# Receptance input in buffers of its own during attention, two probability tiles, and another order of the mixer's first weights

## Chip, cores and metric

The kernel runs on one core of a Trainium2 chip. The metric is the device time of one execution in microseconds (us); several runs give a median. One further execution was profiled.

## What is computed

Three parts follow each other. Attention over 4 batches, 8 heads, 576 positions, head size 64, in which scores more than tau below the row's largest are dropped. A channel mix (RWKV's feed-forward) with 512 and 1024 channels. A spectral mixer: a two-dimensional Fourier transform, its real part added, a layer norm and a two-layer feed-forward with 2048 hidden channels.

```python
scores = scale * np.matmul(q, k.transpose(0, 1, 3, 2))
thresh = np.max(scores, axis=-1, keepdims=True) - tau
attn = softmax(np.where(scores >= thresh, scores, -1e9)) @ v
...
xk = mu_k * x + (1.0 - mu_k) * x_prev      # x_prev: x of the position before
xr = mu_r * x + (1.0 - mu_r) * x_prev
k = np.maximum(xk @ w_k, 0.0)
x = sigmoid(xr @ w_r) * (k * k @ w_v)
...
u = x + real(fft(fft(x, axis=1), axis=2))
out = u + np.maximum(layernorm(u) @ w_ch1, 0.0) @ w_ch2
```

## The kernel before

Attention works on 16 pairs of heads, 4 pairs for each batch, with 9 steps for each pair. A step has scores on TensorE (PE, `s`, L218 and L232), the row's largest on VectorE (DVE, L258), the exponential on ScalarE (ACT, L269), the selection and its sum on DVE (L273), the normalization on GpSimd (POOL, L281), transposes on PE (`t`, L320 and L328, and `tm`, L340 and L343, for the step that holds the remainders), and copies of the transposed probabilities from PSUM into a probability tile `pt` on ACT (L323, L347). A tile `pt` holds one half (288 positions) of a pair; the pool keeps three of them. When a half is complete, the product with the values runs on PE (`av`, L379), and its result becomes a piece of `xT`.

The feed-forward works on halves of a batch: `ffn_stream` is a generator with, for every half, 8 key tiles (`kps`, L399 to L401, 96 matmuls), 4 receptance tiles (`rps`, the same lines, 48 matmuls), 4 value tiles (`vps`, L511 to L513, 96 matmuls), and the transposes of the result of the half before (`xn`, L529), which stand between `kps` and `rps`. Every product is three matmuls, of high and low parts. The inputs are made by `build_xs`: for each of 4 chunks a multiplication on POOL (L423), a multiply-add on DVE (L424, `xtmp`), the high part on ACT (L425, `xh`) and the low part on POOL (L427, `xl`; a few on DVE). There is one buffer each for `xh` and `xl`, and key and receptance inputs take turns in it. The call only queues the chunks in `builds`; they are written into the program two at a time, once in each attention step.

`do_X` pulls the stream in every attention step as far as a credit allows. A scheduler then orders all instructions of each engine by data, buffers and priorities, so the order on an engine is not that of the source. Feed-forward of batches 0 to 2 lies between the steps of attention, that of batch 3 follows attention, beside the Fourier transforms of the first batches and the conversion of the mixer's weights.

The mixer's weights come in four quarters (`quarter`, tiles `cA` and `cB` in turn), each as 8 pieces of `w_ch1` and 8 of `w_ch2`, which are loaded by POOL's queue and split into high and low parts by DVE (L67 to L69), ACT (L72) and POOL (L73). `w_ch1` lies so that a piece holds, for one of four k, the hidden channels of two of four f; product f of `ch1` (`c1ps`, L949 to L951) needs pieces of all four k.

Of the kernel before, what the change touches and what calls it, by code (L numbers as in the profile page):

```python
# [9 lines left out]
F32 = mybir.dt.float32  # L10
F32R = mybir.dt.float32r
# [8 lines left out]
D, FF, FC = 512, 1024, 2048  # L20
HS = S // 2
NPAIR = H // 2
P = dict(PRI=100, SR=1.0, CR=2, ORD=0, PF=0, CB=0, XT=0, XL=0, K2=0, FE=0, FE3=0, MU=0, WP=256, C1=2, RB=4, BB=2, FT=4, A0=[7, 8], A1=[11, 12], B0=[7, 8], B1=[11, 12], PT4=1, OR0='', XH=0, SP0=0, CA=1.48, CN=2.22, QS=1, pF=100, pM=100, pN=100, pT=100, pO=100, pE=100, pS=100, pA=0, pX=0, NA=0, LT=2, WS=3, WR=1, CC=3.0, BN=2, OR='FATXOESBI', TM=8, SO=0, SO0=0, AO=0, AO0=0, QS0=0, XD=0, TH=0, SM=0, SM0=0, N0=34, qF=100, qM=100, qN=100, qT=100, qO=100, qE=100, qS=100, qA=100, qX=30, RQ=[0,0,0,0,0,0,0,0], XN=0, QN=36, AVR=0, LX=2, WD=0, WP2=512, E3=1, NA0=0, W0=0, XD2=0, PO=0, WP1=512, IN=[0,1,2,2,4,5,6,7])
# [5 lines left out]
def tile_kernel(ctx: ExitStack, tc: tile.TileContext, a):  # L29
# [48 lines left out]
    def whole(pair, base=0):  # L78
        return lambda c, n: [x[:, c - base:c - base + n] for x in pair]
# [6 lines left out]
    def big(slot, name):  # L86
        return wA.tile([128, 4096], F32R, tag=slot, name=name)
# [3 lines left out]
    wr = [wC.tile([128, 2048], F32R, name=f"wr{i}") for i in range(2)]  # L91
# [3 lines left out]
    at = astack.enter_context(tc.tile_pool(name="at", bufs=1, side="right"))  # L95
# [32 lines left out]
    def settle():  # L128
        go, second[:] = list(second), []
        for f in go:  # L130
            f()
        while pending:
            pending.pop(0)()
# [4 lines left out]
    heads, vts, ptu, ptr, et, em, sps, stat, xT = ({} for _ in range(9))  # L138
# [128 lines left out]
    def emit_exp(n):  # L267
        st = stat[n]
        act.activation(two(eview(n)), sps[n][:, :, 0:HS], AF.Exp, bias=st[:, 0:1])  # L269
# [27 lines left out]

    def unit(pi, half):
        if (pi, half) not in ptu:
            ptu[pi, half] = at.tile([128, 2, 4, HS], F32, tag="pt", bufs=3, name="pt")  # L300
        return ptu[pi, half]

    def rem_unit(pi, half):
# [66 lines left out]
    xdone = [0, 0]  # L370
# [25 lines left out]
    def proj(ps, w, x, m, width, nk):  # L396
        for k in range(nk):
            wh, wl = (t_[:, k * width + 128 * m:k * width + 128 * m + 128] for t_ in w)
            pe.matmul(ps, wh, x[0][:, k, :], start=(k == 0), stop=False)  # L399
            pe.matmul(ps, wh, x[1][:, k, :], start=False, stop=False)  # L400
            pe.matmul(ps, wl, x[0][:, k, :], start=False, stop=(k == nk - 1))  # L401

    def build_xs(b, half, which):
        fp = ffn["pool"]
        hi = fp.tile([128, 4, HS], F32R, tag="xh", name="xh")
        lo = fp.tile([128, 4, HS], F32R, tag="xl", name="xl")

        def chunk(c):
            x = xT[b, c, half]
            tmp = fp.tile([128, HS], F32, tag="xtmp", bufs=2, name="xtmp")  # L410
            m = 4 * which + c
            if P['XD'] >> (4 * which + c) & 1:
                act.activation(tmp, x[:, 0:HS], AF.Copy, scale=mus[:, 8 + m:9 + m])
                t = lo[:, c, :].bitcast(F32)
                act.activation(t, x[:, 1:], AF.Copy, scale=mus[:, m:m + 1])
                pool.tensor_tensor(tmp, t, tmp, op=ALU.add)
                act.activation(hi[:, c, :], tmp, AF.Copy)
                pool.tensor_tensor(lo[:, c, :], tmp, hi[:, c, :].bitcast(F32), op=ALU.subtract)
                return
            if b == B - 1 and P['XT'] and half + P['XT'] > 1:  # L420
                dve.tensor_scalar(tmp, x[:, 0:HS], mus[:, 8 + m:9 + m], None, op0=ALU.mult)
            else:
                pool.tensor_scalar(tmp, x[:, 0:HS], mus[:, 8 + m:9 + m], 1.0, op0=ALU.mult, op1=ALU.mult)  # L423
            dve.scalar_tensor_tensor(tmp, x[:, 1:], mus[:, m:m + 1], tmp, op0=ALU.mult, op1=ALU.add)  # L424
            act.activation(hi[:, c, :], tmp, AF.Copy)  # L425
            eng = dve if b == B - 1 and (c < P['XL']) else pool
            eng.tensor_tensor(lo[:, c, :], tmp, hi[:, c, :].bitcast(F32), op=ALU.subtract)  # L427

        builds.extend((lambda c=c: chunk(c)) for c in range(4))
        return hi, lo  # L430
# [3 lines left out]
    def ffn_stream():  # L434
        fp = ffn["pool"]
        xt_out = None
        for b in range(B):
            for half in range(2):
                if half == 0:
                    while xdone[P['XH'] == 0] < NPAIR * (b + 1):  # L440
                        yield 0
                    xs = build_xs(b, half, 0)
                while builds:
                    yield 0
                k2 = [fp.tile([128, 8, HS], F32R, tag=f"k2{i}", name=f"k2{i}") for i in range(2)]
                for f in range(8):
                    ps = bank([128, HS], "kps")
# [29 lines left out]
                    yield 1.48  # L477
                if b == B - 1 and half == 1:
                    ffn["k_done"] = True
                xs = build_xs(b, half, 1)  # L480
                if xt_out:
                    yield from xt_out()
                while builds:
                    yield 0
                for _ in state['late']:
                    pass
                t = fp.tile([128, 4, HS], F32, tag="t", name="tg")
                for m in range(4):
                    ps = bank([128, HS], "rps")
                    proj(ps, wr, xs, m, D, 4)  # L490

                    def post(m=m, ps=ps, half=half, t=t):
                        o = t[:, m, ::-1] if half else t[:, m, :]
                        with tc.high_priority(offset=400 if last else 0):
                            act.activation(o, ps, AF.Tanh, scale=0.5)

                    pending.append(post)
                    yield 1.48
                settle()
                settle()  # L500
                if b == B - 1 and half == 1:
                    ffn["r_done"] = True
                if half == 0:
                    while xdone[1] < NPAIR * (b + 1):
                        yield 0
                    xs = build_xs(b, 1, 0)
                for m in range(4):
                    ps = bank([128, HS], "vps")
                    for k in range(8):
# [70 lines left out]
    for n in range(P['LX']):  # L580
        emit_max(n)
        emit_th(n)
        emit_exp(n)
    state = dict(stream=None, credit=0.0, w=0.0, s=P['LX'] + 1, m=P['LX'], e=P['LX'])
    IN = (
        (load_head, 1, (0,)), (conv_k, 1, (0,)), (conv_q, 1, (0,)), (load_v, 0, ()),
        (load_head, 1, (1,)), (conv_k, 1, (1,)), (conv_q, 1, (1,)),
# [107 lines left out]
    for n in range(NSTEP + 8):  # L695
        pi, s = divmod(n, 9)
# [3 lines left out]
            acts[k](n, pi, s)  # L700
    stream = state['stream']
    settle()
    astack.close()


# [7 lines left out]
    fp = fstack.enter_context(tc.tile_pool(name="fft", bufs=1, side="right"))  # L713
# [182 lines left out]
    def quarter(q):  # L896

        t = [big(f"{'AB'[q % 2]}{i}", f"c{'AB'[q % 2]}{i}") for i in range(2)]
        wq[q] = t
        todo = []  # L900
        for k, src in enumerate(("w_ch1", "w_ch2")):
            to = whole([x[:, 2048 * k:2048 * k + 2048] for x in t], 2048 * q)
            todo += [(a[src], to, j) for j in range(8 * q, 8 * q + 8)]
        yield from weight_pieces(todo, None, stage2, 256, rb=3, bb=2)


# [137 lines left out]
    credit = 0.0  # L1044
# [143 lines left out]
```

## Time and profile before

| | |
|---|---|
| median of 3 runs | 1101.86 us (1101.68 to 1103.26) |
| profiled execution, its own time | 1095.96 us |
| its span | 1094.2 us |
| PE busy | 1018.6 us, 93% of the span |
| DVE busy | 684.8 us, 63% |
| ACT busy | 521.4 us, 48% |
| POOL busy | 421.3 us, 39% |
| mean granted TensorE clock | 0.985 |

The span reaches from the first to the last instruction of the profiled execution. Busy time is the time in which an engine works on at least one instruction. Matmuls overlap, so a busy PE isn't always one at its peak. In the views a wait is put down to the instruction that ended last before the waiting one began.

### The profile page before, as it was taken

The numbers are of one execution on the slowest core, as the hardware profiler recorded it, in microseconds if no ns is written. First come the engines' busy times: TensorE is split into PE (matmuls) and PEld (weight loads), VectorE is DVE, ScalarE is ACT, GpSimd is POOL, SyncE is SP. The second block draws the span as 40 slices with busy tenths as digits, with TensorE's granted clock in tenths as the row PEclk, the third lists the DMA queues.
The fourth block names the chain that finished last, engine by engine and source line by source line (L and its number), as shares of the span: only waits on it lengthen the run. The fifth ranks groups of instructions, "written<-read, shape, count | busy, mean of one in ns | idle before, by whom it ended". The sixth has DMA issues, their size and how long they took to land.

```text
span 1094.2 us, 18961 instructions
## 1 busy us (share of the span) xinstructions
PE 1018.6 (93%) x6933; PEld 895.3 (82%) x6933; DVE 684.8 (63%) x1765; ACT 521.4 (48%) x1211; POOL 421.3 (39%) x568
## 2 busy tenths in 40 slices
PE   5887878999989999899999889999999999999998
PEld 4555667978879789788899788998999999999997
DVE  6989878666477585765357688856545948232222
ACT  4767667675575765747365644433332222111111
POOL 1555567364374563645431555310103625010000
PEclk9999999999999999999999789999999999999999
DMA  6433331110221111200443266535333645222221
GB/s 232 154 102 90 119 98 46 59 55 28 70 68 59 45 37 59 80 13 6 119 131 117 86 186 204 176 135 193 120 114 124 205 142 173 96 97 96 97 97 58
DMA packets 41428, 114.53 MB, mean 105 GB/s; under 512 B 6207, under 2 KB 6628, under 8 KB 41336
## 3 DMA queue, kind: packets, MB, share of 16 engines
q1 hardware_dynamic: 27920, 74.43, 21.1%
q0 software_dynamic: 10432, 33.50, 9.4%
q10 hardware_dynamic: 2984, 5.38, 1.4%
q8 instruction: 55, 0.90, 0.3%
q14 instruction: 37, 0.30, 0.1%
HBM read 84.98 MB, written 28.32 MB: 104 GB/s over the span
## 4 chain that ended last, share of the span: by engine, by line
PE 67%; DVE 9%; DMA 7%; ACT 4%; issue 2%; POOL 2%; DVEq 0%; SPq 0%; ACTq 0%; POOLq 0%
PE c1ps L949 6%; PE c1ps L951 6%; PE c1ps L950 6%; PE c2ps L964 6%; PE c2ps L962 6%; PE c2ps L963 6%; PE av L379 5%; PE s L218 3%; PE t L320 3%; PE kps L399 2%; PE kps L401 2%; PE kps L400 2%; PE vps L511 2%; PE vps L512 2%; PE vps L513 2%
## 5 line engine op out<-in xcount | busy, mean ns | idle before, releaser
L955 DVE SCALAR_TENSOR_TENSOR hl<-c1ps,hh 128x256 fp32r<-128x256 f32 x144 | 60.6, 421 | 157.1 <-ACT hh L954 156.6
L954 ACT ACTIVATE hh<-c1ps 128x256 fp32r<-128x256 f32 x144 | 54.7, 381 | 208.1 <-PE c1ps L951 207.5
L258 DVE TENSOR_REDUCE small<-s 128x1 f32<-128x576 f32 x144 | 107.1, 752 | 60.8 <-PE s L218 48.0
L281 POOL TENSOR_SCALAR e<-e,small 128x576 f32<-128x576 f32 x112 | 89.6, 806 | 105.0 <-DVE small L615 81.3
L273 DVE SCALAR_TENSOR_TENSOR e<-s,small,e 128x576 f32<-128x576 f32 x128 | 102.5, 811 | 25.5 <-ACT e L269 24.7
L269 ACT ACTIVATE e<-s,small 128x576 f32<-128x576 f32 x128 | 93.4, 742 | 32.8 <-DVE small L258 30.7
L987 POOL DMA_DIRECT2D ud<-u x54 | 29.4, 545 | 206.0 <-DVE u L986 181.1
L320 PE MATMUL t<-ident,e 128*128 128x128 f32 x512 | 82.2, 276 | 15.7 <-ACT pt L323 5.1
L323 ACT ACTIVATE pt<-t 128x512 f32<-128x512 f32 x128 | 74.6, 598 | 31.4 <-PE t L320 31.0
L949 PE MATMUL c1ps<-ut,cA 128*128 128x256 f32 x288 | 82.4, 286 | 2.7 <-ACT ut L940 2.0
L320 PEld LDWEIGHTS t<-ident,e 128*128 128x128 f32 x512 | 60.7, 141 | 25.8 <-POOL e L281 7.0
L950 PE MATMUL c1ps<-ut,cA 128*128 128x256 f32 x288 | 81.6, 283 | 0.0
L951 PE MATMUL c1ps<-ut,cA 128*128 128x256 f32 x288 | 81.3, 282 | 0.0
L951 PE MATMUL c1ps<-ut,cB 128*128 128x256 f32 x288 | 81.1, 281 | 0.0
L949 PE MATMUL c1ps<-ut,cB 128*128 128x256 f32 x288 | 80.9, 281 | 0.0
L950 PE MATMUL c1ps<-ut,cB 128*128 128x256 f32 x288 | 80.9, 281 | 0.0
L399 PE MATMUL kps<-xh,wk 128*128 128x288 f32 x256 | 78.6, 308 | 0.9 <-ACT relu L457 0.9
L400 PE MATMUL kps<-xl,wk 128*128 128x288 f32 x256 | 76.6, 300 | 0.0
L401 PE MATMUL kps<-xh,wk 128*128 128x288 f32 x256 | 76.4, 300 | 0.0
L511 PE MATMUL vps<-k,wv 128*128 128x288 f32 x256 | 74.2, 305 | 0.5 <-DVE tg L518 0.5
L472 POOL TENSOR_TENSOR k<-relu,k 128x288 fp32r<-128x288 f32 x64 | 53.1, 835 | 52.7 <-ACT k L470 52.4
L512 PE MATMUL vps<-k,wv 128*128 128x288 f32 x256 | 72.1, 299 | 0.0
(236 smaller groups left out, 3118.2 us busy)
## 6 DMA issues: line engine op xcount, KB each, us to landing
u<-ud SPq DMA_DIRECT2D x36, 512.0 KB
wraw<-in_w_ch POOLq DMA_DIRECT2D x64, 256.0 KB, 3.2
rawqk<-in_qk SPq DMA_DIRECT2D x24, 608.0 KB
ud<-u POOLq DMA_DIRECT2D x54, 256.0 KB, 2.5
v<-in_v SPq DMA_DIRECT2D x16, 320.0 KB
un<-ud SPq DMA_DIRECT2D x18, 256.0 KB
out<-u SPq DMA_DIRECT2D x18, 256.0 KB
wraw<-in_w_k SPq DMA_DIRECT2D x8, 512.0 KB
```

The source lines that it names most:

```text
L258: dve.tensor_reduce(st[:, 0:1], sps[n][:, :, 0:HS], axis=AX.XY, op=ALU.max, negate=True)
L269: act.activation(two(eview(n)), sps[n][:, :, 0:HS], AF.Exp, bias=st[:, 0:1])
L273: dve.scalar_tensor_tensor(e, sps[n][:, :, 0:HS], st[:, 1:2], e, op0=ALU.is_ge, op1=ALU.mult, accum_out=st[:, 2:3])
L320: pe.transpose(t[:, k, :], e[:, o + 128 * k:o + 128 * (k + 1)], ident)
L399: pe.matmul(ps, wh, x[0][:, k, :], start=(k == 0), stop=False)
L400: pe.matmul(ps, wh, x[1][:, k, :], start=False, stop=False)
L401: pe.matmul(ps, wl, x[0][:, k, :], start=False, stop=(k == nk - 1))
L511: pe.matmul(ps, wv[0][:, c:c + 128], k2[0][:, k, :], start=(k == 0), stop=False)
L512: pe.matmul(ps, wv[0][:, c:c + 128], k2[1][:, k, :], start=False, stop=False)
L949: pe.matmul(ps, wh, ut[0][:, k, :], start=(k == 0), stop=False)
L950: pe.matmul(ps, wh, ut[1][:, k, :], start=False, stop=False)
L951: pe.matmul(ps, wl, ut[0][:, k, :], start=False, stop=(k == 3))
```

## The change

- The pool of probability tiles has two tiles instead of three.
- While attention's pool is open, the receptance input has a buffer pair of its own (`xh2`, `xl2`) in that pool, and `build_xs` for it is called ahead of the key tiles of the same half. After attention it takes turns with the key input as before, and is built behind the key tiles.
- For the first half of a batch, the test that the second half's attention output is there, and the call that builds the key input of the second half, stand ahead of the receptance tiles instead of behind them.
- The pieces of `w_ch1` are loaded and split in the order 0, 2, 4, 6, 1, 3, 5, 7, so that the pieces for the first two f of all four k come first.

```diff
-            ptu[pi, half] = at.tile([128, 2, 4, HS], F32, tag="pt", bufs=3, name="pt")
+            ptu[pi, half] = at.tile([128, 2, 4, HS], F32, tag="pt", bufs=2, name="pt")
...
     def build_xs(b, half, which):
         fp = ffn["pool"]
-        hi = fp.tile([128, 4, HS], F32R, tag="xh", name="xh")
-        lo = fp.tile([128, 4, HS], F32R, tag="xl", name="xl")
+        p, m = (at, 2) if which and state['at'] else (fp, "")
+        hi = p.tile([128, 4, HS], F32R, tag=f"xh{m}", name="xh")
+        lo = p.tile([128, 4, HS], F32R, tag=f"xl{m}", name="xl")
...
                 while builds:
                     yield 0
+                xs_r = build_xs(b, half, 1) if state['at'] else None
                 k2 = [fp.tile([128, 8, HS], F32R, tag=f"k2{i}", name=f"k2{i}") for i in range(2)]
...
-                xs = build_xs(b, half, 1)
+                xs_r = xs_r or build_xs(b, half, 1)
                 if xt_out:
                     yield from xt_out()
                 while builds:
                     yield 0
+                if half == 0:
+                    while xdone[1] < NPAIR * (b + 1):
+                        yield 0
+                    xs = build_xs(b, 1, 0)
...
-                    proj(ps, wr, xs, m, D, 4)
+                    proj(ps, wr, xs_r, m, D, 4)
...
-                if half == 0:
-                    while xdone[1] < NPAIR * (b + 1):
-                        yield 0
-                    xs = build_xs(b, 1, 0)
...
-    state = dict(stream=None, credit=0.0, w=0.0, s=P['LX'] + 1, m=P['LX'], e=P['LX'])
+    state = dict(at=True, stream=None, credit=0.0, w=0.0, s=P['LX'] + 1, m=P['LX'], e=P['LX'])
...
+    state['at'] = False
     astack.close()
...
-            todo += [(a[src], to, j) for j in range(8 * q, 8 * q + 8)]
+            todo += [(a[src], to, 8 * q + j) for j in ((0, 2, 4, 6, 1, 3, 5, 7) if k == 0 else range(8))]
```

Each engine has the same instructions as before, in another order from the first key tile on. Three places follow; lines behind L402 are shifted by one to three in the changed kernel.

On PE, where the first half of batch 0 goes from key to receptance tiles, before:

```order
L401 MATMUL kps<-xh,wk_85 128x288
L320 MATMUL t<-ident,e 128x128 x8
L399 MATMUL rps<-xh,wr_88 128x288 x2
L218 MATMUL s<-kh,q 128x288 x2
L218 MATMUL s<-kl,q 128x288 x2
L400 MATMUL rps<-xl,wr_88 128x288
L401 MATMUL rps<-xh,wr_89 128x288
```

and in the changed kernel:

```order
L401 MATMUL kps<-xh,wk_85 128x288
L399 MATMUL rps<-xh,wr_88 128x288
L400 MATMUL rps<-xl,wr_88 128x288
L401 MATMUL rps<-xh,wr_89 128x288
L399 MATMUL rps<-xh,wr_88 128x288
L328 MATMUL t_1684<-ident,e 128x128
L400 MATMUL rps<-xl,wr_88 128x288
```

The eight transposes between the two stages and the two scores between receptance matmuls have moved elsewhere.

On PE, around the values' product of pair 13, first half, before; the transposes are those of pair 14 (rows between them, receptance matmuls and scores, are left out):

```order
L401 MATMUL rps<-xh,wr_89 128x288
L320 MATMUL t<-ident,e 128x128 x8
L399 MATMUL rps<-xh,wr_88 128x288
...
L399 MATMUL rps<-xh,wr_88 128x288
L379 MATMUL av<-ptr,v 64x288 x2
L379 MATMUL av<-pt,v 64x288 x8
```

and in the changed kernel:

```order
L515 MATMUL vps<-k_4742,wv_87 128x288
L379 MATMUL av<-ptr,v 64x288 x2
L379 MATMUL av<-pt,v 64x288 x8
L218 MATMUL s<-kh,q 128x288 x2
L218 MATMUL s<-kl,q 128x288 x2
L328 MATMUL t_5414<-ident,e 128x128
L320 MATMUL t<-ident,e 128x128 x4
```

The product now stands ahead of the next pair's first transposes; before, they stood 53 matmuls ahead of its end.

On DVE, at the last products of the feed-forward (`tg`), with conversions of weight pieces (`wbits`) around them, before:

```order
L518 SCALAR_TENSOR_TENSOR tg<-tg,vps 128x288
L765 TENSOR_TENSOR fsol<-fp,fsoh 128x256
L67 TENSOR_SCALAR wbits<-wraw 128x256
L68 SCALAR_TENSOR_TENSOR wbits<-wraw,wbits 128x256
L69 SCALAR_TENSOR_TENSOR wbits<-wraw,wbits 128x256
L67 TENSOR_SCALAR wbits<-wraw 128x256
L518 SCALAR_TENSOR_TENSOR tg<-tg,vps 128x288
```

and in the changed kernel:

```order
L520 SCALAR_TENSOR_TENSOR tg<-tg,vps 128x288
L68 SCALAR_TENSOR_TENSOR wbits<-wraw,wbits 128x256
L761 TENSOR_TENSOR fp<-fp,fq 128x256
L768 TENSOR_TENSOR fsel<-fy,fseh 128x257
L69 SCALAR_TENSOR_TENSOR wbits<-wraw,wbits 128x256
L768 TENSOR_TENSOR fsol<-fp,fsoh 128x256
L67 TENSOR_SCALAR wbits<-wraw 128x256
L520 SCALAR_TENSOR_TENSOR tg<-tg,vps 128x288
```

The first of the two products now stands ahead of steps of the transform (fp, fsel), and no whole conversion of a piece lies between the two.

## Rows read from the trace of the kernel before

**Rows 1.** page part 1: busy us, share of the span, instructions
```profile
PE 1018.6 (93%) x6933; PEld 895.3 (82%) x6933; DVE 684.8 (63%) x1765; ACT 521.4 (48%) x1211; POOL 421.3 (39%) x568
```

**Rows 2.** windows view: stretch, length, busy (instructions) of PE, PEld, DVE, ACT, POOL; PEclk, DMA, GB/s
```profile
0.00:123.00 123.00, 92.34 (x500) 62.93 (x502) 102.01 (x294) 80.19 (x156) 56.58 (x63) 0.97 0.44 144
...
123.00:535.00 412.00, 384.13 (x2880) 339.27 (x2878) 278.36 (x757) 271.56 (x613) 225.29 (x286) 1.00 0.17 52
...
600.00:700.00 100.00, 88.27 (x572) 79.70 (x571) 81.22 (x193) 50.76 (x131) 52.08 (x77) 0.90 0.53 168
...
700.00:1089.00 389.00, 389.00 (x2515) 352.48 (x2513) 182.80 (x414) 86.44 (x222) 66.24 (x111) 1.00 0.37 124
```

**Rows 3.** windows view, fine: handovers and stretches of the feed-forward, columns as above
```profile
123.00:166.00 43.00, 35.78 (x254) 30.00 (x251) 34.80 (x91) 29.22 (x66) 26.70 (x28) 0.96 0.30 94
...
166.00:176.00 10.00, 7.19 (x48) 5.86 (x48) 9.01 (x24) 9.02 (x23) 8.79 (x11) 1.00 0.03 4
...
231.00:243.00 12.00, 9.55 (x72) 7.21 (x71) 8.97 (x22) 9.95 (x25) 9.54 (x14) 1.00 0.32 101
...
243.00:303.00 60.00, 59.22 (x455) 53.33 (x454) 36.76 (x105) 36.48 (x82) 26.62 (x34) 1.00 0.15 49
...
303.00:315.00 12.00, 8.34 (x58) 6.84 (x57) 9.96 (x29) 9.70 (x25) 11.27 (x15) 1.00 0.29 95
...
375.00:388.00 13.00, 10.25 (x74) 8.63 (x73) 10.72 (x25) 12.78 (x31) 12.46 (x16) 1.00 0.27 89
...
445.00:459.00 14.00, 9.80 (x70) 8.37 (x69) 11.25 (x30) 10.84 (x27) 11.89 (x15) 1.00 0.40 128
...
515.00:525.00 10.00, 7.52 (x56) 6.22 (x55) 3.55 (x9) 8.73 (x24) 8.65 (x12) 1.00 0.17 59
```

**Rows 4.** waits view of PE, 123 to 548 us: in total, times, longest
```profile
PE rps L400 <- POOL xl L427: 2.7, 3, 1.4
...
PE xn L529 <- ACT xnat L537: 2.6, 4, 1.0
...
PE rps L399 <- ACT xh L425: 0.4, 1, 0.4
```

**Rows 5.** one line's view (ns min/median/max), then the timeline, DVE and PE
```profile
L424 DVE SCALAR_TENSOR_TENSOR xtmp<-xt,small,xtmp x64: 479/748/1706, 94.0 to 616.3; 128x288 f32<-128x288 f32 x64
...
236.43 1.71 DVE L424 SCALAR_TENSOR_TENSOR xtmp<-xt,small,xtmp 128x288 f32<-128x288 f32 x1
...
239.63 0.82 DVE L273 SCALAR_TENSOR_TENSOR e<-s,small,e 128x576 f32<-128x576 f32 x1
...
240.51 0.54 PE L218 MATMUL s<-kh,q 128*128 128x288 f32 x2 [1.28 <-DVE e L273]
...
309.25 1.55 DVE L424 SCALAR_TENSOR_TENSOR xtmp<-xt,small,xtmp 128x288 f32<-128x288 f32 x1
...
313.24 0.53 PE L218 MATMUL s<-kh,q 128*128 128x288 f32 x2 [1.51 <-DVE xt L366]
```

**Rows 6.** timeline: probability copies (ACT L323) and av matmuls (PE L379)
```profile
256.11 0.61 ACT L323 ACTIVATE pt<-t 128x512 f32<-128x512 f32 x1
...
256.57 2.11 PE L379 MATMUL av<-pt,v 128*64 128x288 f32 x16
...
460.88 1.10 ACT L323 ACTIVATE pt<-t 128x512 f32<-128x512 f32 x2
...
466.08 2.11 PE L379 MATMUL av<-pt,v 128*64 128x288 f32 x16
```

**Rows 7.** one tile's view of L73, then the timeline at the mixer's start
```profile
L73 POOL TENSOR_TENSOR cA<-wbits,cA x16: 727/748/2343, 611.1 to 652.7; 128x256 fp32r<-128x256 f32 x16
...
648.21 1.20 DVE L69 SCALAR_TENSOR_TENSOR wbits<-wraw,wbits 128x256 int32<-128x256 int32 x1
...
649.84 0.77 PE L529 MATMUL xn<-ident,tg 128*128 128x128 f32 x5 [1.84 <-DVE tg L518]
...
653.47 0.58 PE L949 MATMUL c1ps<-ut,cA 128*128 128x256 f32 x1 [2.00 <-ACT ut L940]
```

## The prediction, made before the changed kernel ran

> **What bounds the kernel now.** I began with the page's busy shares: TensorE (PE) is busy 93% of the span, 1018.6 us, so 75.6 us of the span are without a matmul [rows 1]. All matmuls stay, so the time can change only through those 75.6 us, or through the granted clock. The windows view says where they are [rows 2]: 30.7 us in the first 123 us (attention alone, no feed-forward matmul yet), 27.9 us between 123 and 535 us (attention with the feed-forward of batches 0 to 2 between its steps), 11.7 us between 600 and 700 us (end of the feed-forward of batch 3, start of the mixer), none from 700 us to 1089 us; the 5.3 us left over are between 535 and 600 us and at the end.
>
> The middle part I cut finer, at the six places where the stream of the feed-forward goes from its key projection (kps) to its receptance projection (rps) [rows 3]. The long stretches between them are full, as the one from 243 to 303 us, where PE is busy 59.22 of 60 us. The idle time sits in the six short windows: 2.81, 2.45, 3.66, 2.75, 4.20 and 2.48 us, together **18.35 us**. That is the place that the change works on. The stretch before the first of them, 123 to 166 us, has another 7.22 us idle with VectorE (DVE) busy 34.80 of its 43 us.
>
> What PE waits for in this part [rows 4]: 2.7 us for xl and 0.4 us for xh, the two halves of the receptance input; 2.6 us for the copy (xnat) that frees a bank of the output transposes xn; most of the rest for products of attention (selected scores, copied probabilities).
>
> **The receptance input in buffers of its own.** Before, key and receptance inputs share one buffer pair. The receptance input can be written only after the last key matmul, and rps waits for it. Now it is built at the start of the key stage. No instruction is added: four chunks per half of POOL L423, DVE L424, ACT L425, POOL L427 as before, only earlier. In the order of PE the rps of the first half follow the last kps directly, where eight transposes stood between; in five of the six places rps now starts with twelve matmuls in one piece, before in one. So the direct wait of 2.7 + 0.4 = **3.1 us** goes.
>
> What of the other 15.2 us goes? The chunks also hold up attention on DVE. At 236.43 us one xtmp takes 1.71 us; the select (L273) behind it starts at 239.63, and PE waits 1.28 us for it [rows 5]. At 309.25 one takes 1.55 us, and PE waits 1.51 us at 313.24. That is 2.8 us put down to chunks. But the slot that the receptance input leaves is taken at once: the next key input is now asked for before rps, not after, and POOL's order shows xl rows behind the last k rows of a half as before. The window keeps four chunks; only nobody on PE waits for them. I therefore take half, **1.4 us**, bounded by 0 and 2.8. For the remaining 12.4 us I take 0: xn and attention matmuls still stand between kps and rps (201 matmuls over the six places by the order, 214 before), and their waits are of attention itself. The upper bound is all of 12.4.
>
> The chunks moved into the key stage cost DVE and POOL time there. Four chunks are 4 x 0.48 to 4 x 1.71 us of DVE per half [rows 5]. DVE is busy 36.76 of 60 us in such a stretch [rows 3], so 23 us of idle time hide them; I take 0. In 123 to 166 us the cover is thin (8.2 us idle), and the first half could lose up to 4 x 0.75 = 3.0 us there, by the median of xtmp.
>
> Here the Trainium skill speaks against the change: "SBUF — State Buffer", section "Who interferes with whom", says that a VectorE instruction with two SBUF inputs contends with a GpSimd instruction that reads SBUF, and that the later one is blocked for the whole instruction. xtmp has two SBUF inputs, and the key stage is where POOL runs its eight k subtractions. The spread of 0.48 to 1.71 us in [rows 5] agrees. By the rule every moved chunk could pay the longer time; that is rival 4.
>
> **Waiting for the whole batch earlier.** For half 0 the stream now waits for the second half of the batch's attention output before rps, not before vps. Before the key stage of half 0 it has waited for the same count already, so this test never holds. Cost 0. After attention (batch 3) the inputs share the old pair again; PE's order there is the same row for row from the vps of batch 2, half 1, up to the mixer.
>
> **Two probability tiles instead of three.** A tile of (pair, half) may be overwritten only when its av matmuls are done. With three, the trace uses the third at a few places: at 256.11 us a probability copy of pair 8 is written, while av of pair 7, half 0, ends at 258.68; at 460.88 one of pair 14, against 468.19 for av of pair 13 [rows 6]. These are the first and the last of five such overlaps, of 2.6, 1.6, 5.0, 3.0 and 7.3 us, 19.5 us in all; the other 25 turns have slack of 0.4 us or more. The new order puts the av matmuls ahead of these transposes at all places (next pair's first transpose at least six matmuls behind). Price between 0, if feed-forward matmuls fill the place (they stand around it, and PE is full in these stretches), and 19.5 us, if each wait stops PE. I take 0, since [rows 3] shows PE never short of work between the windows.
>
> **Order of the mixer's first weights.** In quarter 0 the last of sixteen pieces is split from 652.7 us on, and the first c1ps matmul starts at 653.47, held by the turned input ut and not by a weight [rows 7]; the pieces of w_ch1 are the first eight of the sixteen. The pieces of the other quarters are read where PE never idles, from 700 us on [rows 2]. So the order of the pieces is worth 0; the cover is the end of the feed-forward, and if it were gone PE would wait for a conversion or two of some 1.2 us, as the DVE part in [rows 7].
>
> **The tail.** On DVE one conversion of a weight piece (L67 to L69) now stands behind the last tg products rather than ahead of them. Before, the last tg waits behind such a conversion and PE waits 1.84 us for it [rows 7]. Bounded by 0 and 1.84; I take half, **0.9 us**. The granted clock was 0.90 of full speed between 600 and 700 us [rows 2], a mix of its two levels 1.2 and 2.4 GHz that is some 10 us of missing clock; PE has the same matmuls in the same order there up to the mixer's first group, so I take no change.
>
> **Sum.** 3.1 + 1.4 + 0.9 = 5.4 us off. The profiled execution took 1095.96 us, 1.76 us around its span of 1094.2; it becomes 1090.6. The median of the runs shown is 5.9 us above the profiled one, and I move the difference onto it: 1101.86 - 5.4 = **1096.5 us**. Two medians of this kernel can be told apart from about 0.2% on, 2.2 us.
>
> **Rivals.**
> 1. *The windows close altogether.* If r work at hand is what PE lacked there, the whole 18.35 us go: 1083.5 us. For it: the stretches with feed-forward work at hand are full. Against: the xn transposes and their copies still stand before rps, and the chunks stay in the window.
> 2. *Nothing that can be measured.* What rps no longer waits for, attention's steps wait for instead, since PE takes its queue in order and these waits were only hidden one behind the other: 1101.9, within 2.2 us. For it: the number of xn and attention matmuls between kps and rps falls by only 6%.
> 3. *The missing third tile stops PE, and the kernel is slower.* The place is the copy of a pair's first probabilities behind the av of the pair before; both transpose banks are then full, and PE's next transpose stands in front of feed-forward work. If half of the 19.5 us reaches PE: 1096.5 + 9.8 = 1106.3; all of it, 1116. It turns the sign when more than 5.4 us, 28% of the overlap, reach PE. Against: the new order has av ahead at all five places.
> 4. *The moved chunks hold up attention in the key stage.* If each of six halves pays one select behind a long xtmp, some 1.4 us as in [rows 5], that is 8.4 us on top of the forecast: 1104.9. By the page on SBUF named above this is what overlapping POOL would do. Against: DVE has 23 us free per half.
>
> **How the numbers follow.** Forecast 0.42, rival 1 or a good part of it (below 1093) 0.18, rival 2 0.20, rival 3 0.13, rival 4 0.07. Faster by over 0.2% is the forecast and rival 1, 0.60; within 0.2% is rival 2, 0.20; slower is rivals 3 and 4, 0.20. The forecast's own range is 1093 to 1099.6. The range for 8 in 10 goes to 1087, about three quarters of the way to the closed windows, and to 1106, where half the overlap reaches PE; the outer parts of rivals 1 and 3 are left out, some 0.15.
>
> **What would show it.** Right: no wait of rps for xl or xh between 123 and 535 us, the windows around the six handovers idle about 14 us instead of 18.35, stretches between them still full, the last av of attention some 4 us earlier, the stretch 700 to 1089 us unchanged in length. Wrong: new waits of transposes for probability copies, or of the copies for av (rival 3); selects behind xtmp in the middle of the key stage (rival 4); waits for xl gone but as much idle time as before (rival 2). It would also be wrong if idle time before 123 us or the clock between 600 and 700 us moved, since I give the change no hold on either.

## The result, and the profile after

The changed kernel took **1084.47 us** (median, 1083.07 to 1085.02), the kernel before, beside it on the same chip, 1101.81 us (1101.68 to 1103.26): a ratio of 0.9838 with a 95% interval of 0.9821 to 0.9855, 17.3 us faster. The prediction gave 1096.5 us with a range from 1087 to 1106. The sign was right; the size was wrong, and the time lies below the range, beside the first rival's 1083.5 us.

The profiled execution of the changed kernel took 1084.79 us, its span 1083.0 us. Page part 1 of it:

```profile
PE 1021.0 (94%) x6933; PEld 900.3 (83%) x6933; DVE 681.6 (63%) x1765; ACT 517.7 (48%) x1211; POOL 425.7 (39%) x568
```

Against [rows 1] PE's time without a matmul fell from 75.6 to 62.0 us (1083.0 - 1021.0), by 13.6 us, and its busy time rose by 2.4 us with the same matmuls (the granted clock is lower than before up to 166 us: 0.93 against 0.97, then 0.91 against 0.96). Together that is the 11.2 us between the two spans. The windows view, cut at the places that answer to [rows 2] and [rows 3] (length, then PE, PEld, DVE, ACT and POOL busy, granted clock, DMA share, GB/s):

```profile
0.00:123.00 123.00, 93.67 (x481) 63.85 (x482) 99.82 (x287) 79.10 (x154) 54.24 (x61) 0.93 0.45 144
...
126.00:166.00 40.00, 35.00 (x232) 28.73 (x231) 35.18 (x92) 29.08 (x65) 33.17 (x36) 0.91 0.32 101
166.00:176.00 10.00, 10.00 (x80) 10.00 (x79) 7.49 (x21) 8.01 (x20) 6.33 (x10) 1.00 0.00 1
176.00:228.00 52.00, 49.99 (x385) 45.26 (x383) 36.73 (x96) 33.55 (x78) 29.90 (x37) 1.00 0.18 55
228.00:240.00 12.00, 11.66 (x93) 9.97 (x92) 7.59 (x23) 9.89 (x23) 6.82 (x10) 1.00 0.25 79
...
298.00:310.00 12.00, 9.82 (x71) 8.23 (x70) 10.78 (x26) 11.56 (x28) 8.94 (x12) 1.00 0.17 52
310.00:361.00 51.00, 51.00 (x395) 46.85 (x394) 33.90 (x92) 32.11 (x72) 26.53 (x34) 1.00 0.18 56
361.00:374.00 13.00, 12.10 (x90) 9.73 (x88) 8.69 (x28) 11.01 (x26) 8.65 (x12) 1.00 0.20 66
...
434.00:448.00 14.00, 12.04 (x87) 10.59 (x86) 11.41 (x31) 10.76 (x26) 13.10 (x17) 1.00 0.29 87
...
503.00:513.00 10.00, 8.52 (x67) 7.80 (x66) 6.23 (x17) 8.36 (x23) 5.14 (x7) 1.00 0.16 58
...
590.00:690.00 100.00, 90.28 (x588) 81.94 (x588) 79.98 (x192) 50.36 (x132) 52.57 (x76) 0.90 0.52 166
690.00:1079.00 389.00, 388.31 (x2506) 351.22 (x2505) 184.37 (x416) 85.59 (x221) 67.13 (x111) 1.00 0.37 125
```

The six handovers idle 0, 0.34, 2.18, 0.90, 1.96 and 1.48 us, together **6.86 us where [rows 3] had 18.35**. The stretches between them are full, as 310 to 361 us, except the first: from 176 to 228 us PE idles 2.01 us, where it idled 0.24 before. Ahead of the first handover, from 126 to 166 us, it idles 5.00 us, against 7.22 from 123 us on in [rows 3]. The mixer is unchanged: 388.31 of 389 us busy, 389.00 in [rows 2].

Who ended PE's waits there. First the kernel before, 123 to 548 us (the lines that [rows 4] left out: in total, times, longest):

```profile
PE s L218 <- DVE e L273: 5.6, 7, 1.3
PE t L328 <- ACT pt L323: 3.1, 4, 1.4
...
PE t L320 <- ACT pt L323: 2.4, 4, 1.3
PE tm L340 <- ACT pt L323: 2.3, 1, 2.3
...
PE rps L399 <- ACT xnat L537: 1.5, 2, 1.2
...
PE t L320 <- ACT pt L347: 0.8, 2, 0.6
```

then the changed one, 126 to 548 us:

```profile
PE kps L399 <- DVE tg L520: 3.3, 2, 2.7
PE s L218 <- DVE e L273: 3.2, 7, 1.0
...
PE rps L399 <- ACT xnat L539: 1.3, 2, 0.8
...
PE t L328 <- ACT pt L323: 1.2, 2, 0.7
...
PE xn L531 <- ACT xnat L539: 0.3, 1, 0.3
```

No rps waits for xl or xh here any more. But most of what went are other waits. Over the whole stretch the transposes (t, tm) waited 8.6 us for ACT's copies of probabilities (3.1 + 2.4 + 2.3 + 0.8), and wait 1.2 us; xn and rps waited 4.1 us for xnat ([rows 4] has the 2.6 of it), and wait 1.6. Of the 8.6 us 3.6 lie ahead of the first handover and 1.1 between handovers. So the six windows are added up by themselves, from the waits view of each:

| in the six windows PE waited for | before, us | after, us | gone, us |
|---|---|---|---|
| receptance input (xl, xh) | 3.1 | 0 | 3.1 |
| copies of probabilities (pt; t, tm) | 3.8 | 0.5 | 3.3 |
| xnat (xn, rps) | 4.1 | 1.6 | 2.5 |
| products of DVE for scores (e, xt, small) | 4.3 | 1.7 | 2.6 |

The other waits there, some 3 us, are as large after as before, so the last column is the 11.5 us that went. One wait is new, 2.7 us of kps for tg from 535 us on, behind the end of attention:

```profile
536.94 0.43 DVE L758 TENSOR_TENSOR fp<-xa,xb 128x255 f32<-128x255 f32 x1 [4.95 <-DMA xb<-xd]
...
538.12 0.40 PE L399 MATMUL kps<-xh,wk 128*128 128x288 f32 x1 [2.75 <-DVE tg L520]
```

The tg product stands on DVE behind a step of the transform (fp) that waited 4.95 us for its loaded input. Before, such a step waited 5.49 us, and PE still had value matmuls for most of it and lost 0.52 us.

### The profile page after: what moved, and what is told of

Its sections match the earlier page's. It is cut to its first block, busy times and chain, and to the rows that moved or that the text cites. A ratio compares the mean times of both kernels' runs of the same rounds, so it can differ in the third digit from the quotient of the medians.

```text
span 1083.0 us, 18967 instructions
## 1 busy us (share of the span) xinstructions
PE 1021.0 (94%) x6933; PEld 900.3 (83%) x6933; DVE 681.6 (63%) x1765; ACT 517.7 (48%) x1211; POOL 425.7 (39%) x568
## 4 chain that ended last, share of the span: by engine, by line
PE 64%; DVE 11%; DMA 6%; ACT 5%; issue 3%; POOL 2%; SPq 0%; DVEq 0%; ACTq 0%
PE c1ps L952 5%; PE c1ps L954 5%; PE c1ps L953 5%; PE c2ps L965 5%; PE av L379 5%; PE c2ps L966 5%; PE c2ps L967 5%; PE s L218 4%; PE t L320 3%; PE kps L399 3%; PE kps L401 2%; PE kps L400 2%; PE vps L513 2%; PE vps L514 2%; PE vps L515 2%
## 5 line engine op out<-in xcount | busy, mean ns | idle before, releaser
L323 ACT ACTIVATE pt<-t 128x512 f32<-128x512 f32 x128 | 74.5, 599 | 24.5 <-PE t L320 24.2
L513 PE MATMUL vps<-k,wv 128*128 128x288 f32 x256 | 76.7, 305 | 0.0
L514 PE MATMUL vps<-k,wv 128*128 128x288 f32 x256 | 76.5, 303 | 0.0
L515 PE MATMUL vps<-k,wv 128*128 128x288 f32 x256 | 75.5, 301 | 0.0
```

What stands on the lines that cost most here:

```text
L513: pe.matmul(ps, wv[0][:, c:c + 128], k2[0][:, k, :], start=(k == 0), stop=False)
L514: pe.matmul(ps, wv[0][:, c:c + 128], k2[1][:, k, :], start=False, stop=False)
L515: pe.matmul(ps, wv[1][:, c:c + 128], k2[0][:, k, :], start=False, stop=(k == 7))
```

## Where a wait went: the fifth handover

PE's timeline of the kernel before (start, length, idle time ahead and what ended it):

```profile
450.96 0.33 PE L328 MATMUL t<-ident,e 128*128 128x128 f32 x1 [1.38 <-ACT pt L323]
451.87 0.63 PE L320 MATMUL t<-ident,e 128*128 128x128 f32 x4 [0.58 <-ACT pt L323]
452.60 0.40 PE L399 MATMUL rps<-xh,wr 128*128 128x288 f32 x1
...
454.85 0.40 PE L400 MATMUL rps<-xl,wr 128*128 128x288 f32 x1 [0.61 <-POOL xl L427]
```

and of the changed one:

```profile
433.41 0.27 PE L320 MATMUL t<-ident,e 128*128 128x128 f32 x1
433.44 0.38 PE L400 MATMUL kps<-xl,wk 128*128 128x288 f32 x1
...
437.05 0.61 PE L531 MATMUL xn<-ident,tg 128*32 128x128 f32 x4 [0.33 <-ACT xnat L539]
438.39 0.66 PE L340 MATMUL tm<-ident,em 128*128 128x128 f32 x4 [0.72 <-POOL em L281]
...
440.42 0.41 PE L399 MATMUL rps<-xh,wr 128*128 128x288 f32 x1 [0.50 <-ACT xnat L539]
440.67 0.29 PE L400 MATMUL rps<-xl,wr 128*128 128x288 f32 x1
```

Before, the transposes of probabilities stood between the last key and the first receptance matmul. PE takes its queue in order, so it stood still for 1.96 us until ACT had copied a bank, and only then came to rps, which waited for xl another 0.61 us. In the changed kernel transposes of probabilities stand among key matmuls, at 433 us, where no wait shows. The handover isn't free of waits: 1.55 us for xnat and em are left in the rows above.

## Experiments

Theory 1: PE had no receptance work at hand at the handovers, because the input stood in a shared buffer. Rivals: the scheduler's order is what counts, whichever buffers there are (2); the empty steps of the stream ahead of rps cost the time (3). An order differs from another where the same instructions stand at other places of an engine's queue.

The table has every run: the median, the difference to the kernel before in the same comparison (its median there was 1100.7 to 1101.5 us), and PE's idle time in the six handovers, here taken from 1 us ahead of the last key matmul to the end of the thirteenth receptance matmul, the first of the second tile (16.9 us before, 6.8 in the changed kernel).

| kernel | median us | to before | handovers idle us |
|---|---|---|---|
| pt2 | 1099.99 | -0.7 | 16.0 |
| hoist | 1102.41 | +1.7 | 16.6 |
| own | 1086.09 | -14.6 | 10.0 |
| own_late | 1094.83 | -5.9 | 12.1 |
| before_now | 1100.50 | -0.8 | 14.8 |
| own_now | 1091.62 | -9.7 | 10.2 |
| own_stall | 1083.77 | -17.5 | 10.1 |
| no_rbuild | 1092.79 | -8.5 | 14.7 |
| before_cn20, after_cn20 | 1092.17, 1091.41 | -8.6, -9.4 | 15.2, 13.0 |
| before_cn205, after_cn205 | 1097.57, 1096.26 | -3.2, -4.5 | 19.3, 16.8 |
| before_cn215, after_cn215 | 1091.87, 1078.66 | -8.9, -22.1 | 14.3, 7.3 |
| before_cn22, after_cn22 | 1090.93, 1076.07 | -9.8, -24.7 | 13.9, 4.4 |
| now_cn22 | 1091.05 | -10.4 | 11.5 |
| after_s4 | 1084.98 | -16.5 | 7.8 |

**The parts.** Two probability tiles alone; and the earlier test and call of the next key input alone:

```diff
-            ptu[pi, half] = at.tile([128, 2, 4, HS], F32, tag="pt", bufs=3, name="pt")
+            ptu[pi, half] = at.tile([128, 2, 4, HS], F32, tag="pt", bufs=2, name="pt")
```

> Only two probability tiles instead of three. The prediction put this at 0, with up to 19.5 us of loss if the five overlaps in the trace of before stop PE. Theory 1: within 2 us of before, the copies wait but PE has key, receptance or value matmuls at hand. The rival (the third tile mattered): 5 to 15 us slower. Theory 2: the order is new here too, so it could also be faster by several us.

> Only the test for the batch's second half and the call for its key input moved ahead of the receptance tiles; shared buffers, three probability tiles, old weight order. Theory 1: the receptance input is still built behind the key tiles in the shared buffer, so the handovers stay idle some 18 us and the time is within 2 us of before. Theory 2: a new order that could gain or lose several us.

Measured: ratios of 0.9995 (0.9976 to 1.0014) and 1.0018 (1.0003 to 1.0034). Neither gains anything. The buffers, with two tiles, without the earlier call and with the old order of weights; then the same with the input called behind the key tiles and the earlier call of the next key input:

```diff
+                xs_r = build_xs(b, half, 1) if state['at'] else None
                 k2 = [fp.tile([128, 8, HS], F32R, tag=f"k2{i}", name=f"k2{i}") for i in range(2)]
...
-                xs = build_xs(b, half, 1)
+                xs_r = xs_r or build_xs(b, half, 1)
```

> Only the receptance buffers of its own with the early build (and the two probability tiles that make room for them); the next key input is asked for behind the receptance tiles as before, the weights come in the old order. Theory 1 (PE lacked receptance work at the six handovers, and the early build puts it at hand): most of the gain of the full change stays, 13 to 17 us below before, and the six windows are idle some 7 us instead of 18.35. Theory 2 (the gain is a lucky order of the scheduler, not the early build): the time can lie anywhere between before and after, with the idle time spread over other places.

> Receptance buffers of its own, but the call that builds the receptance input stays behind the key tiles; the key input of the second half is asked for ahead of the receptance tiles, two probability tiles. Theory 1 in its strict form (it is the early build): the chunks come as late as before, PE still waits for xl at some handovers, and 3 to 8 us are gained. If the free buffer alone is enough, since the scheduler can then write the chunks beside the last key tiles: 12 us or more. Theory 2: anything.

Measured: 0.9868 (0.9847 to 0.989) and 0.9947 (0.993 to 0.9963). So at this credit the buffers carry the gain, and the early call is the larger part of it. But it isn't that the input comes earlier: in own_late too the chunks run as soon as the buffer is free (those of the first half at 124 to 139 us, beside the first key matmuls), and between 126 and 548 us no rps waits for xl or xh, which its expectation had said. What differs is the order. With the late call the transposes still wait for the copies (view of the waits, own_late, 126 to 548 us):

```profile
PE t L328 <- ACT pt L323: 4.9, 5, 1.5
...
PE t L320 <- ACT pt L323: 1.9, 4, 0.9
```

**Empty steps, or work at hand?** Chunks written at once, so that the stream has no empty step ahead of rps, with own buffers and with the shared one; and two empty steps put into own:

```diff
                 xs = build_xs(b, half, 1)
+                while state['at'] and builds:
+                    builds.pop(0)()
```

```diff
+                if state['at']:
+                    yield 0
+                    yield 0
```

> The kernel of own_late (receptance buffers of its own, built behind the key tiles, key input of the second half asked for ahead of the receptance tiles), but the four chunks are written into the program at once, not two per attention step, so that the stream passes no attention step without work between key and receptance tiles. Theory 3 (what costs the time at a handover are the attention steps in which the stream gives PE nothing, since it waits for its queue of chunks to be empty): as good as the early build, 12 to 15 us below before. Theory 1 (the chunks themselves come too late for PE): as own_late, 4 to 8 us below before.

> The kernel before, with shared buffers and three probability tiles, but the four chunks of the receptance input are written into the program at once behind the key tiles. Theory 3: a good part of the gain without any buffer, 5 to 12 us below before, less only the direct wait for xl of some 3 us. Theory 1: within 2 us of before, since the input can't be written before the last key matmul.

> The kernel of own (buffers of its own, early build), with two attention steps put in ahead of the receptance tiles in which the stream gives nothing. Theory 3: the gain of 14.6 us shrinks to that of own_late, some 6 us, though the input is ready early. Theory 1: the input is ready, so the gain stays at 12 to 15 us.

Measured: 0.9908 (0.9884 to 0.9932), 0.9998 (0.9983 to 1.0013) and 0.9846 (0.9828 to 0.9863). Without empty steps the kernel before gains nothing; with two more, own loses nothing. By these two theory 3 fell. The first doesn't fit theory 1 either: 9.7 us lie between its 4 to 8 and the 12 to 15 of theory 3, so with the late call the empty steps may count for some 4 us.

**No receptance input at all.** During attention the receptance product takes the key input, and no chunk is built for it:

```diff
-                xs = build_xs(b, half, 1)
+                xs = xs if state['at'] else build_xs(b, half, 1)
```

> The kernel before, but during attention the receptance input isn't built and the receptance product takes the key input, so for batches 0 to 2 the receptance is that of the wrong mixture: 24 chunks of POOL, DVE and ACT work and every wait for them are gone. It bounds what the receptance input can cost. Theory 1 and theory 3 both: at least the gain of own, 15 us. If the work of the chunks themselves costs nothing on PE: 14 to 18 us. If the chunks also hold up attention by their load: 20 us or more.

Measured: 0.992 (0.9897 to 0.9943), 8.5 us, less than the real change, with 24 chunks fewer. Both theories had said 15 us or more, and both missed. Here the key input keeps the shared buffer through rps, and the next one is built in the value stage. The waits view, 126 to 548 us, shows what is left:

```profile
PE t L320 <- ACT pt L323: 5.8, 3, 3.6
PE tm L340 <- ACT pt L323: 3.6, 2, 2.3
```

So a receptance input that is ready is not enough: with the transposes at such places, their waits stay (10.6 us with the t of L328).

**Other orders of both kernels.** One number of the pacing, the credit that a step gives to the stream, was changed from 2.1 to 2.0, 2.05, 2.15 and 2.2. The instructions stay, their order moves:

```diff
-'CN': 2.1
+'CN': 2.2
```

> The kernel before with one number of the stream's pacing changed: the credit that an attention step gives to the feed-forward is 2.0 instead of 2.1. The instructions are the same, in another order (some 1800 of PE's rows move). Theory 1 (the shared input buffer is what keeps PE short of work at the handovers): the order is not the point, so within some 4 us of the kernel before, 1097 to 1106 us, idle time of the six handovers 14 to 19 us. Theory 2 (the gain of the changed kernel is a lucky order): orders of the same kernel scatter by as much as the gain, so this and the other re-ordered kernels lie anywhere from 1084 to 1102 us, whichever buffers they have.

> The changed kernel with the credit 2.0 instead of 2.1. Theory 1: 1082 to 1092 us, since the receptance input is still ready when the last key matmul ends; at least 8 us below the kernel before with the same credit. Theory 2: anywhere from 1084 to 1102 us, the difference to the kernel before with the same credit of either sign.

> The same with a credit of 2.2. Theory 1: 1097 to 1106 us, transposes wait 6 us or more for copies of probabilities between 123 and 548 us. Theory 2: anywhere from 1084 to 1102 us.

> The changed kernel with the credit 2.2. Theory 1: 1082 to 1092 us, at least 8 us below the kernel before with the same credit; of the time that is over 1084, the waits of transposes for copies of probabilities should hold the larger part. Theory 2: anywhere from 1084 to 1102 us.

> The kernel before with the credit 2.05. Theory 1b (the own buffers save 8 to 15 us at most orders, and each kernel scatters by some 5 us with its order): 1090 to 1104 us, and 5 us or more above the changed kernel at the same credit. Theory 2 (what was measured at 2.1 is the luck of the order): the difference to the changed kernel is of either sign or within 3 us.

> The changed kernel with the credit 2.05. Theory 1b: 1076 to 1092 us, 5 us or more below the kernel before at the same credit, with less idle time in the six handovers than that. Theory 2: within 3 us of it, or above it. Both: the time follows the idle time of the six handovers, 4 to 8 us of it where the time is under 1085 us, over 12 us where it is over 1090 us.

> The kernel before with the credit 2.15. Theory 1b: 1088 to 1104 us, 5 us or more above the changed kernel at the same credit. Theory 2: a difference of either sign or within 3 us.

> The changed kernel with the credit 2.15. Theory 1b: 1076 to 1088 us, 5 us or more below the kernel before at the same credit. Theory 2: within 3 us of it, or above it.

Theory 1 missed at credits 2.0 and 2.2 as it stood: the kernel before itself became 8.6 to 9.8 us faster at three of the four credits, which no buffer explains. The differences between the two kernels, at credits 2.0, 2.05, 2.1, 2.15 and 2.2, are 0.8, 1.3, 17.3, 13.2 and 14.9 us, never of the other sign; the first two aren't clear of the scatter of the runs. So theory 2, within 3 us, held at 2.0 and 2.05 and missed at 2.15 and 2.2. Theory 1b (the buffers save 8 to 15 us at most orders) held at 2.15 and failed at 2.05. At 2.05 the waits have come back in another place (changed kernel, 126 to 548 us):

```profile
PE rps L399 <- ACT xnat L539: 7.3, 5, 3.5
...
PE t L328 <- ACT pt L323: 3.6, 4, 1.9
```

The changed kernel at 2.2 beats both kernels, and all that the theories had said of it: 1076.07 us, a ratio of 0.9776 (0.9756 to 0.9796) to before.

**Place or buffer.** The empty steps had also moved the step of a pair in which the stream gives out the first receptance tile, from steps 4 and 5 to 2, 3 and 4 in the changed kernel, and to 2 and 0 at credit 2.2. Two kernels cross place and buffers: before_now at credit 2.2 (shared buffers, steps 2 and 0), and the changed kernel at credit 2.3 with two empty steps ahead of rps (own buffers, step 4 at all six).

> The kernel before with shared buffers and three probability tiles, the receptance chunks written into the program at once (no empty steps) and the credit 2.2. All six handovers are then pulled in steps 2, 0, 2, 0, 2, 0 of a pair, as in the changed kernel at credit 2.2, which took 1076 us. Place theory: six handovers idle 8 us or less, time 1076 to 1086 us. Buffer theory: the receptance matmuls wait for the shared buffer at this place too, handovers idle 10 us or more, 1088 to 1100 us.

> The changed kernel with its own buffers, credit 2.3 and two empty steps ahead of the receptance tiles, so that all six handovers are pulled in step 4 of a pair. Place theory: handovers idle 12 us or more, 1088 to 1098 us. Buffer theory: as the changed kernel at credits 2.1 to 2.2, handovers idle 4 to 10 us, 1076 to 1085 us.

Measured: 1091.05 us (0.99, 0.9869 to 0.9931) with 11.5 us idle, and 1084.98 us (0.985, 0.9827 to 0.9872) with 7.8 us. Both times lie where the buffer theory put them, and the place theory fell. Shared buffers at the same places and the same credit cost 15.0 us against the changed kernel at 2.2. (The third tile and the late call of the next key input differ too, which alone were worth 0.7 and 1.7 us at credit 2.1, and the order of the weights, which no run took alone.) But the reason that the buffer theory gave didn't show: in the trace of now_cn22 no rps waits for xl or xh between 126 and 548 us. PE waits there for selected scores (6.0 us) and for copies of probabilities by tm (2.6 us), so what the shared buffer costs is again not the direct wait.

Over all orders here, the nine kernels with shared buffers and the whole work took 1090.9 to 1102.4 us, the ten with own buffers 1076.1 to 1096.3, six of them 1086.1 or less.

## Why the prediction was wrong, step by step

- *The direct wait, 3.1 us:* right. It is gone.
- *Attention's waits behind chunks, 1.4 us:* within its bounds of 0 and 2.8. In the six windows scores waited 4.3 us for DVE and wait 1.7, so 2.6 us went. How much of it is the chunks, and how much the order, no run separates.
- *The other 12.4 us of the handovers, put at 0:* **this is the step that failed.** 5.8 us of them went: 3.3 us of transposes that waited for copies of probabilities, and 2.5 us of waits for xnat. With the two steps above, 11.5 of the 18.35 us went, where 4.5 were forecast. The reason given was that these waits "are of attention itself" and that nearly as many matmuls (201 and 214) stand between kps and rps as before. A wait of attention isn't a fixed cost: it costs PE time only if PE has nothing else ahead of the waiting instruction. The count of matmuls didn't ask which of them waits. The transposes waited 3.8 us in the windows and wait 0.5; at the fifth handover they waited 1.96 us, and the ones at 433 us in the changed kernel stand among key matmuls without a wait. The upper bound of 12.4 us was seen, and weighed too low; and own_late and no_rbuild show that the direct wait can go and the transposes' waits stay.
- *The 5.9 us between the profiled execution and the median, moved onto the forecast:* the second step that failed. The profiled span fell by 11.2 us, the median by 17.3, and in the changed kernel the two agree (1084.79 and 1084.47). So the 5.9 us were no constant. Of the 12.0 us between forecast and result, 5.8 lie in the spans (11.2 us instead of 5.4) and 6.2 in this step. The rows behind this are in the last section.
- *Moved chunks, 0:* right in the sum. From the second on PE idles 0.7 us or less in each key stage. In the first, one select stands behind a chunk (141.34 us), and PE waits 0.50 us for it at 143.16, but from 126 to 166 us PE idles less than before. After the change, one line's view (ns min/median/max):

```profile
L425 DVE SCALAR_TENSOR_TENSOR xtmp<-xt,small,xtmp x64: 480/650/1522, 95.4 to 606.5; 128x288 f32<-128x288 f32 x64
```

  [rows 5] had 479/748/1706. By the Trainium skill ("SBUF — State Buffer", section "Who interferes with whom") every moved chunk could have paid the long time beside POOL. The trace of before agrees that POOL is what makes them long: the 18 xtmp that no POOL instruction overlaps took at most 0.53 us, the 42 with 0.2 us or more of overlap 0.49 to 1.71. But after the change the median fell, and rival 4 with its 8.4 us didn't come.
- *The earlier test of the second half, 0:* nearly right; hoist alone was 1.7 us slower, just clear of the scatter. Not foreseen is the new wait of 2.7 us behind attention, where the prediction said that PE's order stays: the order stayed, and the wait came from DVE and a load.
- *Two probability tiles, 0:* right (pt2, -0.7 us). All turns of the two tiles in the changed kernel have a slack of 1.7 us or more, where [rows 6] shows overlaps. Rival 3 fell.
- *Order of the mixer's weights, 0:* nothing in the trace speaks against it, and no run took it alone. The first c1ps waits for ut as in [rows 7], and as long:

```profile
639.38 0.77 PE L531 MATMUL xn<-ident,tg 128*128 128x128 f32 x5 [1.57 <-DVE tg L520]
...
643.01 0.58 PE L952 MATMUL c1ps<-ut,cA 128*128 128x256 f32 x1 [2.00 <-ACT ut L943]
```

- *The tail, 0.9 us:* 0.3 us. PE still waits 1.57 us for the last tg, 1.84 in [rows 7]. In the 100 us around it PE idles 9.72 us, 11.73 in [rows 2]; about half of these 2.0 us lie ahead of the last receptance tiles, and no run explains them.
- *Rival 1* gave nearly the time, by luck: 6.9 of its 18.35 us stayed, and some 6 of the 17.3 us are the offset between profile and median. Its mechanism came true in part at the credits 2.1, 2.15 and 2.2 (6.8, 7.3 and 4.4 us idle are left). *Rival 2*, nothing that can be measured, is what the credits 2.0 and 2.05 show; that waits come back in another place is shown for 2.05.

Of the listed signs, the waits for xl and xh and the unchanged mixer came as said, and the full stretches but for the one from 176 us. The windows idle 6.86 us instead of 14, and the last av ends 12.3 us earlier (525.2 against 537.5 us), not 4. The clock between 600 and 700 us stayed at 0.90 (590 to 690 us now). Idle time before 123 us, which was to stay, went from 30.7 to 29.3 us, at a lower clock.

**What stays open.** Why the buffers gain 13 to 17 us at three credits and 1 us at two. The stream hands out its tiles at 2.05 within a step of where it does at 2.1, and yet the times differ by 11.8 us; the waits of rps for xnat come back there, but no run takes these away alone. So the 17.3 us belong to the buffers together with an order that uses them, and that order was not foreseen by any step of the prediction.

## What to carry to other kernels

When an in-order engine idles at one place for several reasons, do not price only the wait that an edit removes: ask of each neighbouring wait whether other work will stand ahead of the waiting instruction afterwards, and let the range reach to all of them. Where a scheduler sets the order, run both kernels at a few values of a harmless number that re-orders them before crediting an edit with its gain: here that number alone was worth 3 to 10 us for the kernel before, and on top of the change it gave 8.4 us at one value and took 11.8 at another. And compare the granted clock of the profile that the sum is made on with that of the other executions: here it was nearly the highest of all.

## What was not expected: a lower clock at the handovers

The profile of before had the full clock at all six handovers [rows 3]. Others with the same buffers didn't. The windows view of hoist around the third handover:

```profile
304.00:315.30 11.30, 8.66 (x65) 7.50 (x63) 10.31 (x25) 10.67 (x26) 9.89 (x11) 1.00 0.23 78
315.40:318.70 3.30, 3.27 (x15) 3.04 (x14) 2.44 (x8) 2.11 (x5) 2.94 (x5) 0.50 0.78 268
318.80:330.00 11.20, 11.20 (x89) 9.80 (x87) 5.30 (x18) 6.62 (x16) 5.50 (x8) 1.00 0.03 8
```

PE idles 2.6 of 11.3 us at the upper level of 2.4 GHz. Then, with rps at hand and PE busy, the granted clock is 0.50, the lower level of 1.2 GHz, and 15 matmuls run in 3.3 us where the next stretch runs 89 in 11.2 us, some 26 in 3.3. The timeline has it matmul by matmul, 0.24 us apart (0.13 us apart in the changed kernel at 440.67 us and behind):

```profile
316.05 0.44 PE L400 MATMUL rps<-xl,wr 128*128 128x288 f32 x1
316.29 0.44 PE L401 MATMUL rps<-xh,wr 128*128 128x288 f32 x1
316.53 0.44 PE L399 MATMUL rps<-xh,wr 128*128 128x288 f32 x1
```

From 150 to 600 us before has

```profile
150.00:600.00 450.00, 424.97 (x3188) 379.94 (x3187) 293.99 (x807) 285.39 (x662) 228.91 (x301) 1.00 0.20 62
```

and hoist

```profile
150.00:600.00 450.00, 424.85 (x3143) 380.66 (x3142) 288.39 (x792) 279.97 (x652) 228.68 (x299) 0.98 0.20 61
```

PE is as long busy and gets 45 matmuls less done, some 6 us of work at 0.13 us each; hoist's span is 7.1 us longer (1101.3 us). The profiles of pt2, hoist and before_now have 10.2, 17.1 and 17.1 us at the lower level in this stretch, with spans of 1097.5 to 1101.7 us, before none and 1094.2, the changed kernel 3.4.

What the lower level costs is shown: over the twenty profiles PE is busy 1014.0 to 1027.8 us with 6933 matmuls each, 0.37 us more for each us at the lower level in the whole span (31.8 to 58.9 us; correlation 0.86). Where it comes is shown too: between 160 and 540 us the twenty profiles have 36 drops to the lower level, and 33 of them begin in a handover or within 4 us behind one, places that make up a quarter of that time. The three kernels with the least idle time there (4.4, 6.8 and 7.3 us) have none at a handover.

The 5.9 us are shown in part. For 70 executions of before beside the experiments the mean granted clock is on record, without the place: 0.970 to 0.986, half of them at 0.977 or below, in 1096.9 to 1106.6 us. The profile of before had 0.985, and with its 1095.96 us was faster than all of them; that of the changed kernel had 0.977, the lowest of its four. Slower executions of before have the lower clock (correlation -0.65, 3.9 us for each 0.01). By that line the step from 0.977 to 0.985 is worth some 3 us of the 5.9, an estimate; the rest stays open.

That idle time is what brings the drops, and so is paid twice, is argued, not shown. Handover by handover they come in one execution and not in another: before has none with 16.9 us idle, now_cn22 the most, 17.1 us, with 11.5 (correlation of the two over all twenty 0.27). Over all twenty kernels the difference to before falls by 1.7 us for each us of idle time that goes from the handovers (correlation 0.90), but other idle time goes along with it: against all of PE's time without a matmul the slope is 1.4 (0.95).
